# Spectral gated mix on one core: branch weights in 18 strided transfers each, and the l = 512 row placed by one transfer

## The chip, the cores and the metric

The kernel runs on one core of a Trainium2 chip. The metric is the device time of one execution in microseconds (us). Three runs of the kernel before gave 218.82, 219.64 and 219.72 us, median 219.64. The profile is of one execution of 218.76 us, whose instructions span 217.0 us.

## What is computed

Both branches take the same input x of 2048 rows and 1024 columns, in bf16. Each multiplies its 2-D real Fourier transform by its own complex weights (2048 x 513) and transforms back; a gate per row, from x and gate_w, mixes the two results.

```python
g = sigmoid((x * gate_w).sum(-1, keepdims=True))
X = rfft2(A_x)                                  # 2048 x 513 complex
a = irfft2(X * (A_w_r + 1j * A_w_i)).astype(bf16)
b = irfft2(X * (B_w_r + 1j * B_w_i)).astype(bf16)
return g * a + (1 - g) * b
```

## The kernel before, in words

The row index is n = 16 n1 + n2, and a frequency is k = k1 + 128 k2. Real input makes the frequencies k1 and 128 - k1 a pair, so 64 values of k1 are computed. A group `kg` (16 of them) takes four k1, their four mirrors and all 16 k2, which are 128 frequencies, one on each partition. Column frequencies l run from 0 to 512; 512 of them are handled as full rows of 512, and l = 512 on its own.

All instructions are recorded by the class `Sched` in program order, one list for each engine; an instruction waits on the semaphores of what it depends on, by keys of its reads and writes, and each engine works its list strictly in order. Evacuations of PSUM (`ev`, lines 290 to 298) go to ScalarE (ACT) or VectorE (DVE), whichever has the smaller sum of estimated costs so far.

1. Fold and first transform (lines 376 to 404). For each pair of n2, DVE folds the columns of x (`fold`, 8 instructions of 128x1024), TensorE (PE) transforms over n1 with the table F, ACT evacuates into R3 (`Z`). The gate's row sums are collected through R2 and end as the small tile ZG.
2. The first large loop (`for t in range(21)`, lines 524 to 543). At step t, PE runs `stage_d(t)` (columns, table DM), `stage_s2(t-1)` (over n2, result `X` in R4) and `stage_i1(0, t-5)` (inverse over k2 of branch 0). Every second step DVE makes one `prod` (line 443): the complex product of two groups with the branch's weights, two multiplies of 128x2048 and two of 128x1024. At t = 17 and 19 the row l = 512 is handled: `p512` (line 478) multiplies it with column 512 of the weights, which touches every group of the branch, `v512` (line 490) transforms it on PE. At t = 18 and 20 `prod` already works on branch 1. `v512_row(0)` (line 500) follows the loop.
3. The second large loop (lines 558 to 568): `stage_i1(1, t)` of branch 1, its products, `stage_dinv(0, t-3)` (inverse over columns of branch 0), the gate's weights (`gmix`), and at t = 15 `v512_row(1)`.
4. The last loop (lines 598 to 602): `stage_dinv(1, t)` and `s1inv(t-1)`: the last inverse with the mix of both branches, an evacuation, four DVE instructions of 128x512 and the store.

Weights. `wload(b, kgs)` (line 332) fills WR[b] group by group: real and imaginary part, 64 partitions with one row of 513 elements each, and again for the mirror; group 0 needs four transfers of 16 rows for its mirror half because of the row 64. That makes 70 transfers on SyncE's queue (SP) for each branch. In branch 1 every group also writes the keys `zrow` and `gwt`, because WR[1] is the same memory (R2) that the gate used; so each group waits for the group before it. Group kg holds the k1 from 4 kg to 4 kg + 3, at partition 64 pm + 4 k2 + ii (pm is the mirror half, ii the place in the group).

The row l = 512. `v512(b)` leaves its result in V5 as 16 partitions (kg) of 128 elements (16 q2 by 8). It has to stand in partition 0 of VR[b] in the order q2, kg, 8. `v512_row(b)` does that with 16 transfers, one for each kg, after all groups of the branch have been evacuated (`("V", b, k)`). `stage_dinv(b, 0)` waits for it (key `Vf`).

SP's list is, in order: x, the tables, the weights of branch 0, those of branch 1, the tables DI and RM, `v512_row(0)`, `v512_row(1)`, 16 stores.

```python
dma("sp", prs, [], [("W", b, kg)] + (["zrow", "gwt"] if b else []))   # line 352
r = ["X5"] + [("W", b, k) for k in range(16)]                         # line 483, p512
[("V5", b)] + [("V", b, k) for k in range(16)], [("Vf", b)])          # line 503, v512_row
```

Of the kernel before, what the change touches and what calls it, by code (L numbers as in the profile page):

```python
# [7 lines left out]
AP = bass.AP  # L8
BF = dt.bfloat16

NS = 514
# [9 lines left out]
def make_consts():  # L21


    C = {}
    pi2 = 2 * np.pi
    n1 = np.arange(128)[:, None, None]
    n2 = np.arange(16)[None, :, None]
    k1 = np.arange(64)[None, None, :]
    a = pi2 * ((16 * n1 * k1 + n2 * k1) % 2048) / 2048.0
    F = np.zeros((128, 16, 64, 2))  # L30
    F[..., 0] = np.cos(a)
# [34 lines left out]
    for z in range(2):  # L66
        for pm in range(2):
            for k2 in range(16):
                for ii in range(4):
                    i = ii if pm == 0 else 3 - ii  # L70
                    po = pm * 64 + k2 * 4 + ii
                    spec = (z == 1 and i == 0)
                    for q2 in range(16):
                        w = np.exp(-1j * pi2 * q2 * (k2 + (1 if (pm == 1 and not spec) else 0)) / 16)
                        if spec and pm == 1:
                            w = w * np.exp(-1j * pi2 * q2 * 64 / 2048)
                        r0, r1 = q2 * 8 + i * 2, q2 * 8 + i * 2 + 1
                        wr, wi = w.real, w.imag
                        if spec:
                            r = r0 if pm == 0 else r1  # L80
                            S2[z, 0, r, po] = wr
                            S2[z, 1, r, po] = wi
                        else:
                            sg = 1.0 if pm == 0 else -1.0
                            S2[z, 0, r0, po] = wr
                            S2[z, 0, r1, po] = -sg * wi
                            S2[z, 1, r0, po] = wi
                            S2[z, 1, r1, po] = sg * wr
                        cr, ci = wr, -wi
                        K = KI[z, :, po, :, q2, i, :]  # L90
                        if spec:
                            ri = pm
                            K[0, 0, ri], K[1, 0, ri] = cr, -ci
                            K[0, 1, ri], K[1, 1, ri] = ci, cr
                        else:
                            K[0, 0, 0], K[1, 0, 0] = cr, -ci
                            K[0, 0, 1], K[1, 0, 1] = -sg * ci, -sg * cr
                            K[0, 1, 0], K[1, 1, 0] = ci, cr
                            K[0, 1, 1], K[1, 1, 1] = sg * cr, -sg * ci
        S2[z, 2] = -S2[z, 1]  # L100
# [6 lines left out]
    one = np.zeros((128, 2))  # L107
    one[0] = 1.0
    C["ONE"] = one
    return C  # L110


# [118 lines left out]
def bass_gated_mix__spectral_gfnet__spectral_gfnet__prompt_kernel(  # L231
# [24 lines left out]
    RM = sb("RM", 2048)  # L256
    GS = sb("GS", 16)
    ONE = sb("ONE", 2)
    RING = sb("RING", 11264)
    GROW = sb("GROW", 512)  # L260
    X5 = sb("X5", 32)
# [54 lines left out]
        dma(eng, [(ap(t, 0, [[1, n]]).bitcast(dt.uint16), cst[key].ap())], [], [key])  # L316


    XCH = [(0, 2), (2, 4), (4, 8), (8, 12), (12, 16)]
    cload("act", FM, "F", 2048)  # L320
    for a, b in XCH[:2]:
        dma("sp", [(ap(R1, a * 1024, [[1024, b - a], [1, 1024]]), xv[:, a:b, :])], [], [("x", i) for i in range(a, b)])
    dma("act", [(ap(R2, 2048, [[1, 1024]], 0, 1), gate_w.rearrange("(o d) -> o d", o=1))], [], ["gw"])
    cload("act", ONE, "ONE", 2)
    for a, b in XCH[2:]:
        dma("sp", [(ap(R1, a * 1024, [[1024, b - a], [1, 1024]]), xv[:, a:b, :])], [], [("x", i) for i in range(a, b)])
    cload("sp", DM, "DM", 2048)
    cload("sp", S2, "S2", 768)
    cload("sp", KI, "KI", 1024)
    cload("sp", GS, "GS", 16)  # L330

    def wload(b, kgs):
        for kg in kgs:
            prs = []
            T = WR[b]
            for c in range(2):
                src = wsrc[b][c]
                off = kg * 2 * NS + c * NS
                n = src.shape[-1]

                def rows(r0, k2n, inn, p0):
                    return AP(src.tensor, src.offset + r0 * n, [[128 * n, k2n], [n, inn], [1, n]])
                prs.append((ap(T, off, [[1, n]], 0, 64), rows(4 * kg, 16, 4, 0)))
                if kg:
                    prs.append((ap(T, off, [[1, n]], 64, 64), rows(125 - 4 * kg, 16, 4, 64)))
                else:
                    for ii in range(4):
                        r0 = 125 + ii if ii < 3 else 64
                        P = pit[id(T)]
                        prs.append((AP(T, (64 + ii) * P + off, [[4 * P, 16], [1, n]]),  # L350
                                    AP(src.tensor, src.offset + r0 * n, [[128 * n, 16], [1, n]])))
            dma("sp", prs, [], [("W", b, kg)] + (["zrow", "gwt"] if b else []))
    wload(0, range(16))


    def fold(n, src, soff, tmp, st, dst, doff, p0, np_, ns, reads, skey, writes):
# [86 lines left out]
    def prod(b, m):  # L443

        T = WR[b]
        x = ap(R4, 2 * m * 1024, [[1024, 2], [512, 2], [1, 512]])
        w = ap(T, 2 * m * 2 * NS, [[2 * NS, 2], [NS, 2], [1, 512]])
        ws = ap(T, 2 * m * 2 * NS + NS, [[2 * NS, 2], [-NS, 2], [1, 512]])
        r = [("X", 2 * m), ("X", 2 * m + 1), ("W", b, 2 * m), ("W", b, 2 * m + 1)]
        p = PO + m % 2 * 2048  # L450
        dve(1230, tt(ap(RING, TO, [[1024, 2], [512, 2], [1, 512]]), x, w, ALU.mult), r, ["t0"])
        dve(1230, tt(ap(RING, TO + 2048, [[1024, 2], [512, 2], [1, 512]]), x, ws, ALU.mult), r, ["t1"])
        for c, op in enumerate((ALU.subtract, ALU.add)):
            t = TO + 2048 * c
            dve(680, tt(ap(RING, p + c * 512, [[1024, 2], [1, 512]]), ap(RING, t, [[1024, 2], [1, 512]]),
                        ap(RING, t + 512, [[1024, 2], [1, 512]]), op), [f"t{c}"], [("P", m % 2, c)])

    VR = {0: R1, 1: R5}

    def stage_i1(b, kg):  # L460
# [8 lines left out]
        S.op("pe", fns, [("P", kg // 2 % 2, 0), ("P", kg // 2 % 2, 1), "KI"], [("ps", s)])  # L469
        w = [("V", b, kg)]  # L470
        if kg == 0:
            w += allx if b == 0 else [("W", 0, k) for k in range(16)]
        ev(1024, ap(VR[b], kg * 8, [[128, 128], [1, 8]]), pslot(s, 0, [[8, 128], [1, 8]]), [("ps", s)], w)

    def x512():
# [2 lines left out]
    def p512(b):  # L478
# [1 line left out]
        x = ap(X5, 0, [[16, 2], [1, 16]])  # L480
        w = ap(T, 512, [[NS, 2], [2 * NS, 16]])
        ws = ap(T, NS + 512, [[-NS, 2], [2 * NS, 16]])
        r = ["X5"] + [("W", b, k) for k in range(16)]
        dve(100, tt(ap(P5, o, [[16, 2], [1, 16]]), x, w, ALU.mult), r, [("p5", b, 0)])
        dve(100, tt(ap(P5, o + 32, [[16, 2], [1, 16]]), x, ws, ALU.mult), r, [("p5", b, 1)])
        for c, op in enumerate((ALU.subtract, ALU.add)):
# [3 lines left out]
    def v512(b):  # L490
# [6 lines left out]
        S.op("pe", fns, [("P5", b, 0), ("P5", b, 1), "KI"], ["m7"])  # L497
        ev(128, ap(V5, b * 128, [[1, 128]], 0, 16), misc(7, 0, [[1, 128]], 16), ["m7"], [("V5", b)])

    def v512_row(b):  # L500
        dma("sp", [(ap(VR[b], 2048 + 8 * k, [[128, 16], [1, 8]], 0, 1), ap(V5, b * 128, [[8, 16], [1, 8]], k, 1))
                   for k in range(16)],
            [("V5", b)] + [("V", b, k) for k in range(16)], [("Vf", b)])

    def stage_dinv(b, n2):
        s = slot()
# [17 lines left out]
    for t in range(16 + 5):  # L524
# [5 lines left out]
            stage_i1(0, t - 5)  # L530
        if t >= 2 and t % 2 == 0:
            prod(t // 18, t // 2 - 1 - t // 18 * 8)
        if t == 3:
            wload(1, range(16))
            cload("sp", DI, "DI", 2048)
            cload("sp", RM, "RM", 2048)
        if t == 17:
# [95 lines left out]
```

## Time and profile before

| what | value |
|---|---|
| median of three runs | 219.64 us (218.82 to 219.72) |
| profiled execution | 218.76 us, of which 217.0 us span |
| PE, DVE, ACT busy | 60%, 55%, 56% of the span |
| PE weight loads busy | 42% |
| granted TensorE clock, mean | 0.842 of full speed |
| DMA, mean over the span | 90 GB/s |
| chain that ended last | SP issue 19%, DMA of in_B_w_i 17% |

How to read it: the page of the profile cuts the span into 40 slices of 5.4 us. There, PE, DVE and ACT are at eight to ten tenths between slices 8 and 14, stand at 0 from slice 16 to slice 22 (about 81 to 122 us), and are busy again to the end but for a gap at slices 31 and 32. The views by waits, by engine and by time say what each gap waits for. SPq is SP's queue of transfers: a row of it is the time that issuing took, not the time of the data.

### The profile page before, as it was taken

The numbers are of one execution on the slowest core, as the hardware profiler recorded it, in microseconds if no ns is written. First come the engines' busy times: TensorE is split into PE (matmuls) and PEld (weight loads), VectorE is DVE, ScalarE is ACT, GpSimd is POOL, SyncE is SP. The second block draws the span as 40 slices with busy tenths as digits, with TensorE's granted clock in tenths as the row PEclk, the third lists the DMA queues.
The fourth block names the chain that finished last, engine by engine and source line by source line (L and its number), as shares of the span: only waits on it lengthen the run. The fifth ranks groups of instructions, "written<-read, shape, count | busy, mean of one in ns | idle before, by whom it ended". The sixth has DMA issues, their size and how long they took to land.

```text
span 217.0 us, 2645 instructions
## 1 busy us (share of the span) xinstructions
PE 129.6 (60%) x999; PEld 91.4 (42%) x1008; DVE 120.3 (55%) x193; ACT 120.6 (56%) x130; POOL 0.2 (0%) x4
## 2 busy tenths in 40 slices
PE   0368777999999960000000284499799029998970
PEld 0255435666777640000000153388687016665530
DVE  0999900489988870000000399753971203989995
ACT  2258966998998961000000035189999104898870
POOL 0000000000000000000000000000000000000000
PEclk9999999999999985555555558799999856999996
DMA  6999344343112221222222510000000000233243
GB/s 224 354 416 268 97 100 109 85 107 91 36 52 63 61 72 49 66 76 52 62 74 58 194 48 1 3 0 0 0 3 0 1 0 3 97 145 146 100 179 112
DMA packets 15647, 19.55 MB, mean 90 GB/s; under 512 B 3985, under 2 KB 12305, under 8 KB 15250
## 3 DMA queue, kind: packets, MB, share of 16 engines
q1 hardware_dynamic: 15344, 18.85, 28.2%
q10 hardware_dynamic: 290, 0.53, 0.7%
q8 instruction: 8, 0.13, 0.2%
q14 instruction: 5, 0.04, 0.1%
HBM read 15.16 MB, written 4.19 MB: 89 GB/s over the span
## 4 chain that ended last, share of the span: by engine, by line
ACT 24%; DMA 20%; SPq 19%; DVE 17%; PE 12%; issue 7%; DVEq 0%
SPq L313 19%; DMA R<-in_B_w_i_dram 17%; ACT R L296 13%; PE PS L307 12%; DVE RING L310 9%; ACT RING L296 9%; DVE R L310 5%; DMA R<-in_A_x_dram 2%; DVE RING L298 2%; ACT GROW L551 1%; DMA R<-V 1%; ACT L551 1%; DVE P L310 0%; DVEq L209 0%
## 5 line engine op out<-in xcount | busy, mean ns | idle before, releaser
L296 ACT ACTIVATE R<-PS 128x1024 bf16<-128x1024 f32 (+1 forms) x80 | 76.1, 1035 | 27.2 <-PE PS L307 27.2
L310 DVE TENSOR_TENSOR RING<-R 128x2048 bf16<-128x2048 bf16 (+1 forms) x48 | 48.0, 1040 | 14.2 <-ACT R L296 8.4
L296 ACT ACTIVATE RING<-PS 128x1024 bf16<-128x1024 f32 x40 | 43.0, 1133 | 19.6 <-PE PS L307 19.6
L310 DVE TENSOR_TENSOR RING<-RING 128x512 bf16<-128x512 bf16 (+1 forms) x96 | 44.5, 508 | 7.4 <-PE PS L307 4.1
L307 PE MATMUL PS<-DI,R 128*128 128x256 bf16 x256 | 35.3, 286 | 16.6 <-DMA R<-V 9.3
L307 PE MATMUL PS<-KI,RING 128*128 128x256 bf16 x256 | 36.6, 294 | 5.2 <-DVE RING L310 3.2
L307 PEld LDWEIGHTS PS<-DI,R 128*128 128x128 bf16 x256 | 25.4, 102 | 25.4 <-issue 15.8
L307 PEld LDWEIGHTS PS<-KI,RING 128*128 128x128 bf16 x256 | 25.2, 105 | 13.2 <-DVE RING L310 4.0
L307 PE MATMUL PS<-KI,P 128*16 128x128 bf16 (+1 forms) x8 | 1.2, 303 | 42.2 <-DVE P L310 42.2
L310 DVE TENSOR_TENSOR P<-X,R 128x32 bf16<-128x32 bf16 x4 | 0.7, 212 | 43.0 <-DMA R<-in_B_w_i_dram 43.0
L296 ACT ACTIVATE V<-PS 16x128 bf16<-16x128 f32 x2 | 0.5, 258 | 42.1 <-PE PS L307 42.1
L307 PE MATMUL PS<-FM,R 128*128 128x128 bf16 x128 | 11.6, 263 | 13.3 <-DVE R L310 13.3
L307 PEld LDWEIGHTS PS<-KI,P 128*16 128x16 bf16 (+1 forms) x8 | 0.6, 109 | 42.8 <-issue 42.8
L307 PE MATMUL PS<-DM,R 128*128 128x256 bf16 x128 | 16.5, 273 | 0.3 <-ACT RING L296 0.2
L307 PE MATMUL PS<-RING,S 128*128 128x1 bf16 (+2 forms) x91 | 15.8, 304 | 1.3 <-ACT RING L296 1.1
L298 DVE CAST RING<-PS 128x1024 bf16<-128x1024 f32 x8 | 10.0, 1248 | 11.6 <-PE PS L307 11.6
L307 PEld LDWEIGHTS PS<-FM,R 128*128 128x128 bf16 x128 | 9.9, 120 | 15.1 <-DVE R L310 14.7
L307 PEld LDWEIGHTS PS<-DM,R 128*128 128x128 bf16 x128 | 11.8, 98 | 3.0 <-ACT RING L296 1.1
L307 PEld LDWEIGHTS PS<-RING,S 128*128 128x128 bf16 x96 | 7.8, 97 | 7.5 <-ACT RING L296 1.4
L310 DVE TENSOR_TENSOR R<-RING 128x1024 bf16<-128x1024 bf16 x16 | 10.3, 688 | 0.3
L307 PE MATMUL PS<-R,FM 128*128 128x512 bf16 x30 | 9.4, 388 | 0.7 <-ACT RING L296 0.4
L307 PE MATMUL PS<-RING,DM 128*128 128x512 bf16 x30 | 9.4, 391 | 0.1
(23 smaller groups left out, 37.3 us busy)
## 6 DMA issues: line engine op xcount, KB each, us to landing
out_dram<-RING SPq DMA_DIRECT2D x16, 256.0 KB, 2.0
R<-in_A_x_dram SPq DMA_DIRECT2D x3, 1024.0 KB, 10.9
R<-in_A_w_r_dram SPq DMA_DIRECT2D x31, 64.1 KB, 2.3
R<-in_A_w_i_dram SPq DMA_DIRECT2D x31, 64.1 KB, 2.3
R<-in_B_w_r_dram SPq DMA_DIRECT2D x31, 64.1 KB, 2.2
R<-in_B_w_i_dram SPq DMA_DIRECT2D x31, 64.1 KB, 2.2
R<-in_A_x_dram SPq DMA_DIRECT2D x2, 512.0 KB, 5.5
FM<-c_F ACTq DMA_DIRECT2D x1, 512.0 KB, 4.8
```

The lines of the kernel that those rows point to most:

```text
L296: S.op("act", lambda e: e.activation(outap, inap, ACT.Copy), reads, writes)
L298: S.op("dve", lambda e: e.tensor_copy(outap, inap), reads, writes)
L307: return lambda e: e.matmul(o, l, r, start=start, stop=stop, skip_group_check=True)
L310: return lambda e: e.tensor_tensor(out=o, in0=a, in1=b, op=op)
L313: S.op(eng, [lambda e, d=d, s=s: e.dma_start(d, s) for d, s in pairs], reads, writes, dma=kind)
L551: S.op("act", lambda e: e.activation(ap(GROW, 0, [[1, 512]]), misc(7, 0, [[1, 512]]), ACT.Sigmoid), ["m7"], ["GROW"])
```

## The change

- Weights: one recorded transfer group for each branch, made of 18 transfers. For each partition place in a block of eight (pm, ii) and each of real and imaginary part, one transfer fills 16 partitions (one for each k2, eight apart) with all 16 groups: 16 x 16 rows of 513 elements. The place pm = 1, ii = 3 is split in two, because of the row 64. The key is now `("W", b)` for a whole branch: a product of two groups waits for all of it. The keys `zrow` and `gwt` are written once.
- To make that a regular stride, group kg now holds the k1 kg, kg + 16, kg + 32 and kg + 48, and the partition is 8 k2 + 4 pm + ii. The tables F, RM, S2 and KI are permuted accordingly; sizes and counts of matmuls stay.
- The row l = 512: after V5, eight small matmuls with an identity (ID) and one more evacuation bring it to V6, as 16 partitions (q2) of 128 elements, for each branch; then one transfer places it.
- F moves from ACT's queue to SP's, behind the first transfer of x. `wload(1)` is recorded at t = 0 and not at t = 3.

```diff
-    k1 = np.arange(64)[None, None, :]
+    kord = (np.arange(16)[:, None] + 16 * np.arange(4)[None, :]).reshape(-1)
+    k1 = kord[None, None, :]
...
-                    po = pm * 64 + k2 * 4 + ii
+                    po = k2 * 8 + pm * 4 + ii
...
+    xload(0, 2)
+    cload("sp", FM, "F", 2048)
...
-    wload(0, range(16))
+    cload("sp", ID, "ID", 16)
+
+    def wload(b):
+
+        prs = []
+        T = WR[b]
+        P = pit[id(T)]
+        for pm in range(2):
+            for ii in range(4):
+                for c in range(2):
+                    src = wsrc[b][c]
+                    n = src.shape[-1]
+
+                    def part(r0, step, k0, k1):
+                        prs.append((AP(T, (4 * pm + ii) * P + (2 * k0 + c) * NS, [[8 * P, 16], [2 * NS, k1 - k0], [1, n]]),
+                                    AP(src.tensor, src.offset + r0 * n, [[128 * n, 16], [step * n, k1 - k0], [1, n]])))
+                    if pm == 0:
+                        part(16 * ii, 1, 0, 16)
+                    elif ii < 3:
+                        part(80 + 16 * ii, -1, 0, 16)
+                    else:
+                        part(127, -1, 1, 16)
+                        part(64, 1, 0, 1)
+        dma("sp", prs, [], [("W", b)] + (["zrow", "gwt"] if b else []))
+    wload(0)
...
-        r = [("X", 2 * m), ("X", 2 * m + 1), ("W", b, 2 * m), ("W", b, 2 * m + 1)]
+        r = [("X", 2 * m), ("X", 2 * m + 1), ("W", b)]
...
+        fns = [mm(misc(7, j * 16, [[1, 16]], 16), ap(V5, b * 128 + j, [[8, 16]], 0, 16), ap(ID, 0, [[1, 16]], 0, 16), True, True)
+               for j in range(8)]
+        S.op("pe", fns, [("V5", b), "ID"], ["m7"])
+        ev(128, ap(V6, b * 128, [[1, 8], [8, 16]], 0, 16), misc(7, 0, [[16, 8], [1, 16]], 16), ["m7"], [("V6", b)])
+
     def v512_row(b):
-        dma("sp", [(ap(VR[b], 2048 + 8 * k, [[128, 16], [1, 8]], 0, 1), ap(V5, b * 128, [[8, 16], [1, 8]], k, 1))
-                   for k in range(16)],
-            [("V5", b)] + [("V", b, k) for k in range(16)], [("Vf", b)])
+        dma("sp", [(ap(VR[b], 2048, [[128, 16], [1, 128]], 0, 1), ap(V6, b * 128, [[1, 128]], 0, 16))],
+            [("V6", b)] + [("V", b, k) for k in range(16)], [("Vf", b)])
...
-        if t == 3:
-            wload(1, range(16))
+        if t == 0:
+            wload(1)
```

How the order of instructions moves, at three places. First SP, where the weights of branch 1 begin; s_pe is PE's semaphore, s_d28 and s_d29 are those of the first two groups of branch 1. Before:

```order
L313 DMA R<-in_A_w_i_dram 64x1x513 x2
L313 DMA R<-in_B_w_r_dram 64x1x513 [waits s_pe]
L313 DMA R<-in_B_w_r_dram 16x513 x4
L313 DMA R<-in_B_w_i_dram 64x1x513
L313 DMA R<-in_B_w_i_dram 16x513 x4
L313 DMA R<-in_B_w_r_dram 64x1x513 [waits s_d28]
L313 DMA R<-in_B_w_r_dram 64x1x513
L313 DMA R<-in_B_w_r_dram 64x1x513 [waits s_d29]
```

And now, from the end of branch 0 to the start of branch 1:

```order
L319 DMA R<-in_A_w_r_dram 16x15x513
L319 DMA R<-in_A_w_r_dram 16x513
L319 DMA R<-in_A_w_i_dram 16x15x513
L319 DMA R<-in_A_w_i_dram 16x513
L319 DMA R<-in_B_w_r_dram 16x16x513 [waits s_pe]
L319 DMA R<-in_B_w_i_dram 16x16x513
L319 DMA R<-in_B_w_r_dram 16x16x513
```

The wait for PE stays; the 15 waits of a group for the one before it are gone.

Second PE, at the row l = 512 (P holds its products, V its transform), between `stage_i1(0, 14)` and `stage_i1(0, 15)`. Before:

```order
L307 MATMUL PS<-KI,P 16x128 [waits s_dve]
L307 MATMUL PS<-KI,P 16x128
L307 MATMUL PS<-KI,P 1x128 x2
L307 MATMUL PS<-KI,P 16x128 [waits s_dve,s_act]
L307 MATMUL PS<-KI,RING 128x256 x8
```

And now:

```order
L313 MATMUL PS<-KI,P 16x128 [waits s_dve]
L313 MATMUL PS<-KI,P 16x128
L313 MATMUL PS<-KI,P 1x128 x2
L313 MATMUL PS<-ID,V 16x16 [waits s_d12,s_act]
L313 MATMUL PS<-ID,V 16x16 x7
L313 MATMUL PS<-KI,P 16x128 [waits s_dve,s_act]
L313 MATMUL PS<-ID,V 16x16 [waits s_act]
L313 MATMUL PS<-KI,RING 128x256 x8
```

PE, which works in order, waits for two more evacuations by ACT in each branch before it comes to `stage_i1(0, 15)`.

Third DVE, at the start of the last loop; a CAST is an evacuation that fell to DVE. Before:

```order
L310 TENSOR_TENSOR DM<-RM,FM 128x512
L298 CAST R<-PS 128x1024
L298 CAST RING<-PS 128x1024
L310 TENSOR_TENSOR RING<-RING 128x512
L310 TENSOR_TENSOR RING<-RING 128x2x256 x3
L298 CAST RING<-PS 128x1024
```

And now:

```order
L316 TENSOR_TENSOR DM<-RM,FM 128x512
L304 CAST R<-PS 128x1024
L304 CAST RING<-PS 128x1024 x2
L316 TENSOR_TENSOR RING<-RING 128x512
L316 TENSOR_TENSOR RING<-RING 128x2x256 x3
```

The two added evacuations shift the balance of `ev`: two evacuations of the last loop stand ahead of DVE's first block of four, and three instead of four stand behind it.

## Rows read from the trace of the kernel before

**Rows 1.** Waits of the run: engine, line, waited for, us in total, times, longest
```profile
DVE P L310 <- DMA R<-in_B_w_i_dram: 43.0, 1, 43.0
...
PE PS L307 <- DMA R<-V: 9.3, 1, 9.3
```

**Rows 2.** DVE in time, around the products of l = 512: start, us, instruction
```profile
122.87 0.34 DVE L310 TENSOR_TENSOR P<-X,R 128x32 bf16<-128x32 bf16 x2 [42.95 <-DMA R<-in_B_w_i_dram]
...
123.34 2.35 DVE L310 TENSOR_TENSOR RING<-R 128x2048 bf16<-128x2048 bf16 x2
```

**Rows 3.** SP's queue in time: first weights of branch 1, and the table behind them
```profile
51.93 3.14 SPq L313 DMA_DIRECT2D R<-in_B_w_r_dram  x5
...
121.24 0.58 SPq L313 DMA_DIRECT2D DI<-c_DI  x1
```

**Rows 4.** SP's issues of line 313: count, ns least/median/most, first and last start
```profile
L313 SPq DMA_DIRECT2D R<-in_A_w_r_dram x35: 582/594/1384, 5.4 to 49.6; - x35
...
L313 SPq DMA_DIRECT2D R<-V x32: 497/589/592, 127.1 to 175.8; - x32
```

**Rows 5.** DMA issues: count, KB each, median us from issue to landing
```profile
R<-in_B_w_r_dram SPq DMA_DIRECT2D x31, 64.1 KB, 2.2
...
KI<-c_KI SPq DMA_DIRECT2D x1, 256.0 KB, 13.9
...
R<-in_B_w_r_dram SPq DMA_DIRECT2D x4, 16.0 KB, 2.3
```

**Rows 6.** Stretches of time: busy by engine, then PEclk, DMA share, GB/s
```profile
4.00:5.00 1.00, 0.00 (x0) 0.00 (x0) 0.00 (x0) 0.00 (x0) 0.00 (x0) 1.00 1.04 422
...
19.00:20.00 1.00, 1.00 (x7) 0.42 (x6) 1.00 (x3) 1.00 (x2) 0.00 (x0) 1.00 1.27 201
...
26.00:30.00 4.00, 2.82 (x31) 1.74 (x29) 1.52 (x3) 3.69 (x5) 0.00 (x0) 1.00 0.43 103
```

**Rows 7.** DVE in time: the first fold, and the first product of branch 0
```profile
5.78 1.29 DVE L310 TENSOR_TENSOR RING<-R 128x1024 bf16<-128x1024 bf16 x2 [5.78 <-DMA R<-in_A_x_dram]
...
40.90 2.36 DVE L310 TENSOR_TENSOR RING<-R 128x2048 bf16<-128x2048 bf16 x2 [6.41 <-ACT R L296]
```

**Rows 8.** PE and ACT in time, where the first large loop meets the second
```profile
80.80 0.60 PE L307 MATMUL PS<-KI,P 128*16 128x128 bf16 x4
...
124.08 1.89 PE L307 MATMUL PS<-KI,RING 128*128 128x256 bf16 x8
...
138.34 1.86 PE L307 MATMUL PS<-DI,R 128*128 128x256 bf16 x8 [5.57 <-issue]
...
140.24 1.02 ACT L296 ACTIVATE R<-PS 128x1024 bf16<-128x1024 f32 x1 [6.37 <-PE PS L307]
```

**Rows 9.** Groups by line, kept apart by form: count, busy us, mean ns
```profile
L307 PE MATMUL PS<-ONE,R 1*128 1x1 bf16 x24 | 0.9, 160 | 0.7 <-ACT R L296 0.7
...
L296 ACT ACTIVATE V<-PS 16x128 bf16<-16x128 f32 x2 | 0.5, 258 | 42.1 <-PE PS L307 42.1
...
L298 DVE CAST RING<-PS 128x1024 bf16<-128x1024 f32 x8 | 10.0, 1248 | 11.6 <-PE PS L307 11.6
```

**Rows 10.** SP and PE in time, where the second large loop meets the last
```profile
127.06 10.05 SPq L313 DMA_DIRECT2D R<-V  x16
...
165.55 2.88 PE L307 MATMUL PS<-DI,R 128*128 128x256 bf16 x24 [0.27 <-ACT R L296]
...
166.44 9.98 SPq L313 DMA_DIRECT2D R<-V  x16
...
177.69 3.57 PE L307 MATMUL PS<-DI,R 128*128 128x256 bf16 x16 [9.26 <-DMA R<-V]
```

**Rows 11.** The chain that ended last, its piece between SP's last issue and PE
```profile
175.82 1.73 DMA R<-V
```

**Rows 12.** DVE's first block of the last loop, and the stretch from there
```profile
183.91 1.55 DVE L310 TENSOR_TENSOR RING<-RING 128x512 bf16<-128x512 bf16 x4 [1.38 <-ACT RING L296]
...
183.91:214.04 30.13, 24.62 (x160) 15.43 (x161) 28.16 (x68) 23.62 (x25) 0.00 (x0) 0.99 0.34 126
```

More of the change, by code (lines that the diff above doesn't have):

```diff
@@ L109, in make_consts @@
     C["ONE"] = one
+    idt = np.zeros((128, 16))
+    idt[:16] = np.eye(16)
+    C["ID"] = idt
     return C
@@ L258, in bass_gated_mix__spectral_gfnet__spectral_gfnet__prompt_kernel @@
     ONE = sb("ONE", 2)
+    ID = sb("ID", 16)
+    V6 = sb("V6", 256)
     RING = sb("RING", 11264)
@@ L316, in cload, with xload @@
         dma(eng, [(ap(t, 0, [[1, n]]).bitcast(dt.uint16), cst[key].ap())], [], [key])
-    XCH = [(0, 2), (2, 4), (4, 8), (8, 12), (12, 16)]
-    cload("act", FM, "F", 2048)
-    for a, b in XCH[:2]:
+    def xload(a, b):
         dma("sp", [(ap(R1, a * 1024, [[1024, b - a], [1, 1024]]), xv[:, a:b, :])], [], [("x", i) for i in range(a, b)])
+    xload(0, 2)
+    cload("sp", FM, "F", 2048)
     dma("act", [(ap(R2, 2048, [[1, 1024]], 0, 1), gate_w.rearrange("(o d) -> o d", o=1))], [], ["gw"])
     cload("act", ONE, "ONE", 2)
-    for a, b in XCH[2:]:
-        dma("sp", [(ap(R1, a * 1024, [[1024, b - a], [1, 1024]]), xv[:, a:b, :])], [], [("x", i) for i in range(a, b)])
+    for a, b in ((2, 4), (4, 8), (8, 12), (12, 16)):
+        xload(a, b)
     cload("sp", DM, "DM", 2048)
@@ L330, in bass_gated_mix__spectral_gfnet__spectral_gfnet__prompt_kernel @@
     cload("sp", GS, "GS", 16)
[L332 to L352, printed above, removed]
-    wload(0, range(16))
+    cload("sp", ID, "ID", 16)
[20 more added lines that the diff above has]
+    wload(0)
     def fold(n, src, soff, tmp, st, dst, doff, p0, np_, ns, reads, skey, writes):
@@ L471, in stage_i1 @@
         if kg == 0:
-            w += allx if b == 0 else [("W", 0, k) for k in range(16)]
+            w += allx if b == 0 else [("W", 0)]
         ev(1024, ap(VR[b], kg * 8, [[128, 128], [1, 8]]), pslot(s, 0, [[8, 128], [1, 8]]), [("ps", s)], w)
@@ L482, in p512 @@
         ws = ap(T, NS + 512, [[-NS, 2], [2 * NS, 16]])
-        r = ["X5"] + [("W", b, k) for k in range(16)]
+        r = ["X5", ("W", b)]
         dve(100, tt(ap(P5, o, [[16, 2], [1, 16]]), x, w, ALU.mult), r, [("p5", b, 0)])
```

## The prediction

> **What bounds the kernel now.** I read the list of waits first [rows 1]. One wait stands out: DVE sits idle for 43.0 us, once, for a transfer of B's imaginary weights. DVE in time shows the place [rows 2]: the products of the row l = 512 for branch 1 start at 122.87, after 42.95 us of idle time, so DVE had been free since 79.92. These small products need column 512 of all sixteen groups of B's weights, and the large products of branch 1 stand behind them on DVE. SP's queue says why the weights are late [rows 3]: B's 70 transfers are issued from 51.93 to 121.24, 69.3 us. One issue takes a median of 0.594 us [rows 4], 0.63 with the gap to the next; 70 of them are 44 us, and the other 25 us are the 15 waits of a group for the landing of the one before. They begin at 51.93 because A's 70 issues stand ahead.
>
> Then I looked where PE idles afterwards. The first place is 5.57 us ahead of the first inverse over columns of branch 0, at 138.34 [rows 8]; SP issues the 16 small transfers of the l = 512 row just then, from 127.06 to 137.11 [rows 10]. The second is 9.26 us at 177.69, where the trace names that transfer itself [rows 1, 10]. From 183.91 DVE is busy 28.16 of 30.13 us [rows 12]: it bounds the last loop. So three stretches wait for issues on SP, and the rest is compute.
>
> **The change part by part.** All times are on the clock of before, against the profiled execution: 218.76 us, of which 217.0 are span.
>
> *Start.* The first fold waits until 5.78 for x [rows 7], while 0.52 MB of x and 0.52 MB of F travel together from two queues. With F behind that part of x, x lands earlier by at most F's 0.52 MB at 422 GB/s [rows 6], 1.25 us. Folds bound this phase, so all of it moves: -1.2; bounds 0 and -1.25.
>
> *A's weights.* 18 issues replace 70, but the first product now needs the whole branch, 2 x 2048 x 513 x 2 B = 4.20 MB. It starts at 40.90 now, 39.7 after the gain above [rows 7]. What stands ahead in the queue lands at 18.3 (KI, issued at 4.41, takes 13.9 [rows 5]). For the rate there are two rows [rows 6]: a trickle of 103 GB/s keeps the DMA engines busy 0.43 of the time, which scales to 240 GB/s; the short backlog at 19 to 20 us moves 201 GB/s at a share over 1. That gives 17.5 to 20.9 us and A's weights at 35.8 to 39.2. I take 0; the cover is 0.5 to 3.9 us, and if it is gone the delay goes through, since the inverse of branch 0 follows the first product on PE at once. Bounds 0 and +7 (150 GB/s; see the rivals). SP's issues hide behind the data unless one takes over (35.8 - 6.2) / 18 = 1.6 us; no row has 256 rows in one transfer, those there take 0.59 [rows 4]. ID's and F's issues on SP, under 0.6 us each, are hidden with them.
>
> [...]
>
> *B's weights.* They wait for the same PE instruction, now reached as soon as A's issues end (about 18 us) and that instruction is done, before 34. Their data follow A's, 17.5 to 20.9 us more: 53 to 60. DVE comes for them at 78.7. The whole 42.95 us go: **-42.95**. Bounds: 18 us of margin, so nothing less unless the rate is below about half of what I take. DI and RM follow at 65 and are needed after 90.
>
> *The added transposes.* For each branch eight tiny matmuls (0.16 us each at most [rows 9], overlapped: 0.4 us for eight) and an evacuation of 0.26 us [rows 9], with two hand-overs between PE and ACT. PE passes them in order, ahead of the last inverse group of branch 0. From the start of the first l = 512 transform at 80.80 [rows 8] I count: transform to 81.4, V at 82.1 (ACT is busy until then), transposes and V6 to 82.85, second transform and V to 83.8, second transposes to 84.3. That group begins at 84.4, where the old one, shifted by 42.95, would begin at 124.08 - 42.95 = 81.13 [rows 8]: 3.3 us later. DVE's second product of branch 1 reaches the buffer which that group frees at 86.2, so DVE loses nothing.
>
> *Row l = 512 of branch 0.* The last group is evacuated by 87.3; one issue and landing take 1.73 from the start of the issue [rows 11], so the row stands at 89.1, before PE asks at about 92. The 5.57 us of idle time go, the 3.3 us of delay come in: 2.3 us. [...] The evacuation at 140.24, 97.29 when shifted, comes at 92 to 93: **-4.8**; bounds -2.3 and -6.4 (the whole of ACT's 6.37 [rows 8]). From there on ACT bounds the loop, as before.
>
> *Row l = 512 of branch 1.* SP starts at 166.44 [rows 10]; the last of its 16 issues starts at 175.82 [rows 11]. One transfer lands at 168.2, when PE ends the batch begun at 165.55 (168.43 [rows 10]). The 9.26 us go. [...] One evacuation of 1.25 us [rows 9] moves from behind DVE's first block to ahead of it, where it partly replaces ACT's; DVE bounds what is behind [rows 12]. I take 0.5 of it: **-11.5**; bounds -9.3 and -12.3.
>
> *Sum.* -1.2 - 42.95 - 4.8 - 11.5 = -60.45: 218.76 becomes 158.3. The median of the runs is 0.9 above the profiled execution, so I say **159.0**.
>
> **The rivals.**
>
> 1. *A's weights are late.* The wait for a whole branch takes the place of sixteen early ones. It decides below 4.20 MB / (39.7 - 18.3) = 196 GB/s. At 150 GB/s A lands at 46.3 and the time is 165.6; at 175, 161.6. For it: the 201 GB/s of the backlog [rows 6]. Against it: that second mixes large and small rows. Chance 0.20, at 161 to 167.
>
> 2. *The second half gives less.* Between the loops ACT and DVE may hold what PE gains, and the added hand-overs may cost more. With the lower bounds of both terms, -2.3 and -9.3, and nothing at the start, the time is 218.76 - 54.55 = 164.2. Chance 0.12.
>
> 3. *Slower: a transfer of 16 partitions is dealt to few DMA engines.* 240 GB/s over 16 engines is 15 GB/s for one. Two branches of 4.20 MB on k engines take 560/k us after 18.3, and from B's landing the rest is 217 - 122.87 less the 16.3 of the last two terms, 78 us, with 1.8 outside the span. It is slower than before when 560/k exceeds 121, so for four engines or fewer: 238 us at k = 4, some 660 at one. For it: nothing in these rows excludes it for 16 rows, since 16 KB land in 2.3 us [rows 5] and one engine would need only 1.1. Against it: 64 KB land in 2.2 [rows 5] where one engine would need 4.3, so such transfers are spread, and the 16-row ones differ only in the count. Chance 0.04. [...]
>
> 4. *The wait for B's weights stays in other words*, because something orders the transfers still. The new order on SP has one wait ahead of B's 18, for PE, and none between them. Chance 0.01, at about 202.5, the two row terms alone (218.76 - 16.3).
>
> **How the numbers follow.** My case has 0.63, at 155.5 to 161. The range 155.5 to 166.0 takes it with rival 2 and most of rival 1; left out are what is quicker than the bounds, very late weights, and rivals 3 and 4, under 0.2 together. A measurement of this kernel can tell about 0.5% from no change. Faster by more than that: 0.95; within it 0.01; slower 0.04 (rival 3).
>
> **What would show it.** In the list of waits DVE's 43.0 us for in_B_w_i is gone, and so are PE's 9.3 us for V. SP issues 36 weight transfers of about 0.6 us, B's from about 33 us. The first 128x2048 product stands at 39.7 and is released by ACT; if it is released by a transfer of in_A_w, rival 1 holds, and its idle time is the price. The first column inverse of branch 0 follows its predecessor without a gap, as does that of branch 1. The mean clock rises over 0.842. A wait of DVE for B's weights, however short, makes the part on B wrong; transfers that land one engine at a time make all of it wrong.

## The result, and the profile after

The changed kernel ran in 161.62 us (median of four runs, 160.53 to 165.54) beside 219.58 us for the kernel before. The ratio is 0.735, with a 95% interval from 0.728 to 0.741; the ratios here leave out executions that were slower at a lower granted clock, such as that of 165.54 us. The forecast was 159.0, with a range from 155.5 to 166.0. The profiled execution took 160.53 us, of which 159.0 are span; the mean granted clock rose from 0.842 to 0.968.

The list of waits of the changed kernel (engine, line, waited for: us in total, times, longest) no longer has either row of [rows 1]. A new one stands near its head:

```profile
DVE RING L316 <- DMA R<-in_A_w_i_dram: 10.2, 1, 10.2
```

DVE in time (start, us, instruction, and in brackets the idle time before it with what ended it) shows where that wait is, what became of the one for B, and the start:

```profile
4.32 1.29 DVE L316 TENSOR_TENSOR RING<-R 128x1024 bf16<-128x1024 bf16 x2 [4.32 <-DMA R<-in_A_x_dram]
...
8.17 1.29 DVE L316 TENSOR_TENSOR RING<-R 128x1024 bf16<-128x1024 bf16 x2 [1.23 <-DMA R<-in_A_x_dram]
...
44.59 2.36 DVE L316 TENSOR_TENSOR RING<-R 128x2048 bf16<-128x2048 bf16 x2 [10.21 <-DMA R<-in_A_w_i_dram]
...
82.37 0.34 DVE L316 TENSOR_TENSOR P<-X,R 128x32 bf16<-128x32 bf16 x2
...
82.83 0.34 DVE L316 TENSOR_TENSOR P<-X,R 128x32 bf16<-128x32 bf16 x2
```

Branch 1's products of l = 512 stand at 82.83 instead of 122.87 [rows 2], right behind those of branch 0 and without a wait. But the first large product, at 40.90 and released by ACT before [rows 7], is now at 44.59 and released by A's weights. The first fold is 1.46 us earlier than in [rows 7], and the second pair of folds, behind it, now waits for x. Before, it did not:

```profile
8.31 1.28 DVE L310 TENSOR_TENSOR RING<-R 128x1024 bf16<-128x1024 bf16 x2
```

So only 0.14 us is left of that gain.

SP's queue in time shows the issues that [rows 3] and [rows 10] showed before:

```profile
6.34 0.68 SPq L319 DMA_DIRECT2D R<-in_A_w_r_dram  x1
7.06 3.66 SPq L319 DMA_DIRECT2D R<-in_A_w_i_dram  x1
...
34.19 0.57 SPq L319 DMA_DIRECT2D R<-in_B_w_r_dram  x1
...
56.74 0.58 SPq L319 DMA_DIRECT2D DI<-c_DI  x1
...
90.34 30.31 SPq L319 DMA_DIRECT2D R<-V  x2
```

B's issues run from 34.19 to 56.7, where they ran from 51.93 to 121.24. The two transfers of the l = 512 row replace 32 (the last line spans both, at 90.34 and about 120.1). The first A transfer issues in 0.68 us and the second in 3.66, though both have 256 rows. A's 18 issues run from 6.34 to 32.45, 26.1 us; their 4.20 MB take 24.9 at the rate below, so on the whole the issues go at about the pace of the data.

The stretch in which the weights travel says how fast that is (columns as in [rows 6]: busy by engine, PEclk, DMA share, GB/s):

```profile
20.00:40.00 20.00, 16.31 (x151) 9.88 (x151) 7.50 (x13) 15.07 (x18) 0.00 (x0) 1.00 1.14 169
```

That is 169 GB/s with the DMA engines busy throughout (a share of 1.14). Last, PE in time at the l = 512 row, and the clock in the same stretch:

```profile
82.51 1.05 PE L313 MATMUL PS<-KI,RING 128*128 128x256 bf16 x8 [1.96 <-DVE RING L316]
...
84.82 0.43 PE L313 MATMUL PS<-ID,V 16*16 16x16 bf16 x8 [0.94 <-ACT V L302]
86.06 0.59 PE L313 MATMUL PS<-KI,P 128*16 128x128 bf16 x4 [0.82 <-ACT V L302]
87.01 0.43 PE L313 MATMUL PS<-ID,V 16*16 16x16 bf16 x8 [0.36 <-ACT V L302]
87.37 6.15 PE L313 MATMUL PS<-KI,RING 128*128 128x256 bf16 x40
93.36 1.04 PE L313 MATMUL PS<-DI,R 128*128 128x256 bf16 x8
...
119.23 4.67 PE L313 MATMUL PS<-DI,R 128*128 128x256 bf16 x40 [0.26 <-ACT R L302]
```

```profile
82.00:84.00 2.00, 1.37 (x12) 0.90 (x12) 2.00 (x10) 0.40 (x1) 0.00 (x0) 0.97 0.00 0
84.00:86.00 2.00, 0.43 (x8) 0.34 (x8) 2.00 (x3) 1.48 (x3) 0.00 (x0) 0.50 0.00 0
...
88.00:90.00 2.00, 2.00 (x11) 1.40 (x10) 1.75 (x3) 0.91 (x2) 0.00 (x0) 0.50 0.00 0
90.00:92.00 2.00, 2.00 (x17) 1.63 (x16) 2.00 (x4) 1.38 (x3) 0.00 (x0) 0.82 0.02 2
```

Neither the first inverse over columns (93.36, 5.57 us of idle time in [rows 8]) nor the batch of 40 that contains the start of branch 1's (119.23, 9.26 us in [rows 10]) waits for the row. But three hand-overs between PE and ACT, 0.94, 0.82 and 0.36 us, stand between the tiny matmuls, and the granted clock falls there to 0.50 from about 84 to 90. The kernel before has no transposes, and its clock falls at this place too, right behind the same pause of PE for DVE:

```profile
79.52 1.35 PE L307 MATMUL PS<-KI,RING 128*128 128x256 bf16 x8 [1.96 <-DVE RING L310]
```

```profile
80.00:85.00 5.00, 1.39 (x10) 0.63 (x7) 0.00 (x0) 1.17 (x2) 0.00 (x0) 0.51 0.26 67
```

### The profile page after: what moved, and what is told of

The parts are those of the page before. It is cut to its first block, busy times and chain, and to the rows that moved or that the text cites. A ratio compares the mean times of both kernels' runs of the same rounds, so it can differ in the third digit from the quotient of the medians.

```text
span 159.0 us, 2541 instructions
## 1 busy us (share of the span) xinstructions
PE 124.6 (78%) x1015; PEld 90.0 (57%) x1024; DVE 120.4 (76%) x193; ACT 121.7 (77%) x132; POOL 0.2 (0%) x4
## 4 chain that ended last, share of the span: by engine, by line
ACT 37%; PE 27%; DVE 22%; issue 7%; DMA 4%; SPq 1%; DVEq 0%
PE PS L313 27%; ACT R L302 21%; ACT RING L302 13%; DVE RING L316 12%; DVE R L316 6%; DMA R<-in_A_x_dram 4%; DVE RING L304 4%; ACT GROW L564 1%; ACT L564 1%; ACT V L302 1%; SPq L319 1%; DVEq L213 0%
## 5 line engine op out<-in xcount | busy, mean ns | idle before, releaser
L313 PE MATMUL PS<-KI,RING 128*128 128x256 bf16 x256 | 34.0, 281 | 7.5 <-issue 3.1
L313 PE MATMUL PS<-DI,R 128*128 128x256 bf16 x256 | 32.7, 273 | 1.5 <-DVE RING L304 1.2
L313 PEld LDWEIGHTS PS<-KI,RING 128*128 128x128 bf16 x256 | 24.3, 101 | 14.0 <-issue 3.9
L313 PEld LDWEIGHTS PS<-DI,R 128*128 128x128 bf16 x256 | 24.4, 98 | 8.4 <-DVE RING L304 2.2
L313 PE MATMUL PS<-R,G 128*1 128x512 bf16 x32 | 7.5, 378 | 0.7 <-ACT R L302 0.7
L304 DVE CAST R<-PS 128x1024 bf16<-128x1024 f32 x4 | 4.9, 1223 | 3.1 <-PE PS L313 3.1
L313 PEld LDWEIGHTS PS<-RING,DM 128*128 128x128 bf16 x32 | 3.1, 98 | 3.8
```

Source lines behind the costliest of these rows:

```text
L304: S.op("dve", lambda e: e.tensor_copy(outap, inap), reads, writes)
L313: return lambda e: e.matmul(o, l, r, start=start, stop=stop, skip_group_check=True)
```

## The experiments

Three things needed a test: why A's weights come at 169 GB/s, what each part of the change is worth, and what the hand-overs on PE cost. "First product" is the first 128x2048 instruction on DVE that reads A's weights; each span is set against the profiled one of 159.0 unless another is named. The experiments ran on three chips, and where no range of times is given it is one execution. Beside them the kernel before took 219.29 to 222.16 us, so a difference of one or two us between spans of different chips shows little by itself.

**Loading A in two halves.** Branch A is loaded as groups 0 to 7, then 8 to 15, each with its own key, so that the first product waits for half.

```diff
-        dma("sp", prs, [], [("W", b)] + (["zrow", "gwt"] if b else []))
+        for h in (range(2) if b == 0 else (None,)):
...
+            keys = [("W", b, 0), ("W", b, 1)] if h is None else [("W", b, h)]
+            dma("sp", prs, [], keys + (["zrow", "gwt"] if b else []))
```

> Branch 0's weights in two recorded loads (groups 0 to 7, then 8 to 15; 34 transfers of 16 partitions by 8 groups), so that a product waits for half a branch only. Theory (the whole-branch wait for A's weights costs what the first product of branch 0 lost, 44.59 against some 40.8): the first half lands at about 18.3 + 2.1 MB / 168 GB/s = 31, the first product starts at 40.5 to 41 and is released by ACT, and the profiled span falls by 3.5 to 4 us from 159.0, to 155 to 155.5. Rival (the lateness is made up later, because DVE has slack in that loop): the first product moves, the span stays within 1 us of 159. Second rival (36 issues by 16 more cost as much again): the first half lands after 40.5.

Measured: 158.62 us (158.20 to 159.10), ratio 0.719 [0.717, 0.721], span 157.3. The first product is released by ACT again, so the wait for the whole branch did cause the delay:

```profile
41.10 2.36 DVE L316 TENSOR_TENSOR RING<-R 128x2048 bf16<-128x2048 bf16 x2 [6.42 <-ACT R L302]
```

Yet the end comes only 1.7 us earlier, not the 3.5 of the product (the spans of the four executions are 156.4 to 157.3). The clock and PE in time of this kernel show why, next to the rows above:

```profile
80.00:82.00 2.00, 1.73 (x12) 0.88 (x9) 2.00 (x8) 0.76 (x1) 0.00 (x0) 0.55 0.00 0
...
88.00:90.00 2.00, 2.00 (x11) 1.44 (x10) 2.00 (x3) 1.02 (x1) 0.00 (x0) 0.50 0.02 2
```

```profile
79.73 1.47 PE L313 MATMUL PS<-KI,RING 128*128 128x256 bf16 x8 [1.95 <-DVE RING L316]
81.13 0.59 PE L313 MATMUL PS<-KI,P 128*16 128x128 bf16 x4
82.46 0.43 PE L313 MATMUL PS<-ID,V 16*16 16x16 bf16 x8 [0.74 <-ACT V L302]
...
85.02 7.17 PE L313 MATMUL PS<-KI,RING 128*128 128x256 bf16 x40
92.02 1.04 PE L313 MATMUL PS<-DI,R 128*128 128x256 bf16 x8
```

The clock falls earlier, at 80 instead of 84, and is still at 0.50 until 90. It falls behind the pause of 1.95 us, within the batch of 79.73 and ahead of the first hand-over. That batch is 2.78 us earlier than in the changed kernel, the first inverse over columns only 1.34: the same 40 matmuls take 7.17 us instead of 6.15, and about half of the gain is returned in this stretch.

**What sets the rate: order, partitions, alignment.** Four kernels change only how the weights are addressed; the second and the fourth leave them at other frequencies than they belong to, so they serve for the times alone. The first alternates the two mirror halves, so that a transfer to partitions 8 k2 + ii is followed by one to 8 k2 + 4 + ii:

```diff
-        for pm in range(2):
-            for ii in range(4):
-                for c in range(2):
+        for ii in range(4):
+            for c in range(2):
+                for pm in range(2):
```

> The same 18 transfers in another order: the two mirror halves (pm) alternate, so that neighbouring transfers lie on partitions that differ in bit 2. [...] Theory pieces (168 GB/s is what pieces of 1026 bytes give at full load): 167 GB/s and 44.6 stay in any case.

The second loads the same bytes by transfers of 128 partitions with two rows each:

```diff
+        for c in range(2):
...
+                prs.append((AP(T, (4 * h + c) * NS, [[P, 128], [2 * NS, 2], [1, n]]),
+                            AP(src.tensor, src.offset + 2 * h * n, [[16 * n, 128], [n, 2], [1, n]])))
```

> [...] Changed in the computation: the weights stand at other frequencies than they belong to. [...] Theory pieces: 167 GB/s as before, first product at 44 to 45.

The third leaves the transfers and makes the pitch of a row in the tile 528 elements, a multiple of 32 bytes:

```diff
-NS = 514
+NS = 528
```

> The rows of the weights stand 528 elements apart in SBUF and not 514, so that each piece starts at a multiple of 32 bytes there; sources, transfers and counts as in the changed kernel. [...]

The fourth puts each transfer's 16 partitions next to each other:

```diff
-                        prs.append((AP(T, (4 * pm + ii) * P + (2 * k0 + c) * NS, [[8 * P, 16], [2 * NS, k1 - k0], [1, n]]),
+                        prs.append((AP(T, (4 * pm + ii) * 16 * P + (2 * k0 + c) * NS, [[P, 16], [2 * NS, k1 - k0], [1, n]]),
```

> As the changed kernel, sources, counts and pieces the same, but each transfer fills 16 adjacent partitions and not 16 that are eight apart. Changed in the computation: the weights stand at other frequencies than they belong to. [...] Theory source (168 GB/s is due to the sources, 16 places 131 KB apart in memory): 168 GB/s stays, span 159 to 160.

The stretch from 20 to 40 us for alternating halves:

```profile
20.00:40.00 20.00, 17.38 (x146) 9.61 (x146) 7.57 (x13) 13.99 (x17) 0.00 (x0) 1.00 1.13 208
```

For 128 partitions, two shorter stretches, one with A's weights on the way and one with B's (from 20 to 40 there is a pause between them):

```profile
20.00:25.00 5.00, 4.78 (x43) 2.61 (x42) 4.93 (x9) 3.46 (x5) 0.00 (x0) 1.00 1.10 349
...
42.00:48.00 6.00, 5.51 (x43) 3.34 (x43) 5.39 (x7) 6.00 (x8) 0.00 (x0) 1.00 1.10 353
```

For 16 adjacent partitions, the same stretch, and DVE at the first product:

```profile
20.00:40.00 20.00, 17.61 (x145) 9.58 (x144) 7.97 (x14) 13.99 (x17) 0.00 (x0) 1.00 1.14 100
```

```profile
62.77 2.36 DVE L316 TENSOR_TENSOR RING<-R 128x2048 bf16<-128x2048 bf16 x2 [27.26 <-DMA R<-in_A_w_i_dram]
```

The share is 1.10 to 1.14 in all of them, so the DMA engines are equally occupied and the bytes are not. With the pitch of 528 it is 167 GB/s (a share of 1.13), the first product at 44.90 and the time 160.83: this alignment has no part in it. The source rows of the adjacent kernel are those of the changed one, so 100 against 169 comes from the destination's partitions alone. For the 349 to 353 of 128 partitions that is not separated, because its source rows lie differently too. (The adjacent kernel took 181.38 us.) Alternating halves gave 159.51 us with the first product at 41.53, released by ACT; 128 partitions gave 158.51 with it at 40.99. Those two and the halves end within 1.5 us of each other in span (158.0, 156.5, 157.3), and behind the first product they differ in little: it stands at 40.99 to 41.53 in all three.

So at about the same share the rate was 100, 169 or 349 to 353 GB/s; what in the hardware makes the difference is not shown. The two sets of alternating halves lie four partitions apart, and alternating them gained 23% (208 against 169). Why it is 208 and not 350 stays open.

**The l = 512 row.** First the changed kernel with the old 16 transfers for each branch, without V6 and its transposes:

```diff
-        dma("sp", [(ap(VR[b], 2048, [[128, 16], [1, 128]], 0, 1), ap(V6, b * 128, [[1, 128]], 0, 16))],
-            [("V6", b)] + [("V", b, k) for k in range(16)], [("Vf", b)])
+        dma("sp", [(ap(VR[b], 2048 + 8 * k, [[128, 16], [1, 8]], 0, 1), ap(V5, b * 128, [[8, 16], [1, 8]], k, 1))
+                   for k in range(16)],
+            [("V5", b)] + [("V", b, k) for k in range(16)], [("Vf", b)])
```

> The row l = 512 again by 16 transfers for each branch, without the transposes and V6; the weights as in the changed kernel. Theory (the two row terms are worth what the profile of the change shows, 94.1 us from the branch-1 products of l = 512 to the end before, 76.2 now, 17.9 less): PE waits 4 to 6 us ahead of the first column inverse of branch 0 and about 9 us ahead of that of branch 1, and the profiled span is 174 to 177. Rival (most of what came behind the weights is PE's clock, which no longer falls to its lower level for 40 us): the span is 165 to 170.

Measured: 182.63 us, span 180.9, so undoing the row costs 21.9 us, more than either theory said. PE in time of this kernel:

```profile
100.96 1.87 PE L313 MATMUL PS<-DI,R 128*128 128x256 bf16 x8 [7.30 <-issue]
102.61 1.91 PE L313 MATMUL PS<-KI,RING 128*128 128x256 bf16 x8
...
141.49 3.57 PE L313 MATMUL PS<-DI,R 128*128 128x256 bf16 x16 [9.55 <-DMA R<-V]
```

Both waits of [rows 8, 10] are back, the first longer than before (7.30 against 5.57), and with them the batches of 8 at a granted clock of 0.50 (100 to 105), in 1.87 and 1.91 us instead of 1.04. Its l = 512 products of branch 1 stand at 84.19, 1.4 us later than in the changed kernel, which is part of the 21.9. From there to the end it takes 180.9 - 84.2 = 96.7 us.

The clock falls in this kernel too, which has no transposes and one hand-over here, but for about 3 us and not 7:

```profile
86.18 0.59 PE L313 MATMUL PS<-KI,P 128*16 128x128 bf16 x4 [0.94 <-ACT V L302]
```

```profile
86.00:88.00 2.00, 1.82 (x11) 1.23 (x12) 2.00 (x3) 0.39 (x2) 0.00 (x0) 0.50 0.00 0
```

Then the other way round: the kernel before with this part alone.

> The kernel before with its 70 weight transfers for each branch, and only the l = 512 row changed: transposes, V6 and one transfer. Theory (the row terms hold by themselves): span 217.0 - 16 to 18 = 199 to 201, DVE still waits about 43 us for B's weights. Rival (as undoing the row showed, it is worth 21.9): span 195.

Measured: 201.56 us, span 199.8, or 17.2 less than before. DVE still waits for B, somewhat longer than in [rows 2]:

```profile
124.32 0.34 DVE L315 TENSOR_TENSOR P<-X,R 128x32 bf16<-128x32 bf16 x2 [44.66 <-DMA R<-in_B_w_i_dram]
```

From there to the end it takes 199.8 - 124.3 = 75.5 us, where the kernel before takes 217.0 - 122.9 = 94.1 and the changed one 159.0 - 82.8 = 76.2. So from these products on the part is worth 18.6 us in the kernel before, and 96.7 - 76.2 = 20.5 in the changed one. The products stand 1.4 us later in this kernel and in the one with the old row, which makes 17.2 of the first and 21.9 of the second.

**The 15 waits of B's groups.** The kernel before, with only group 0 writing the shared keys:

```diff
-            dma("sp", prs, [], [("W", b, kg)] + (["zrow", "gwt"] if b else []))
+            dma("sp", prs, [], [("W", b, kg)] + (["zrow", "gwt"] if b and kg == 0 else []))
```

> The kernel before, 70 transfers for each branch, but only the first group of branch 1 writes the keys zrow and gwt, so the 15 waits of a group for the one before it are gone and the issues remain. Theory (44 us of issue and 25 us of waits add up): B's issues end at 52 + 70 x 0.634 = 96.4, the products of l = 512 for branch 1 start at 98 to 99 and not at 122.9, the span is 192 to 194. [...]

Measured: 196.20 us, span 194.4. DVE in time:

```profile
100.05 0.34 DVE L310 TENSOR_TENSOR P<-X,R 128x32 bf16<-128x32 bf16 x2 [20.27 <-DMA R<-in_B_w_i_dram]
```

The wait shrinks from 42.95 to 20.27 us, and the span by 22.6, to a little above the 192 to 194 of the theory. The data do not bound it now: B's issues run from 52.1 to 98.2 at about 0.6 us each, and the DMA engines are busy less than half of the time (a share of 0.42 from 70 to 80 and 0.47 from 80 to 90). (Beside this run the kernel before took 222.16 us, 26.0 more than this one; the wait in the trace, 22.7 shorter, speaks for the smaller figure.) So of the change's 58.0 us of span, 22.6 need only this one condition. The step from there to 18 transfers gives 13.5 (194.4 to 180.9, the experiment with the old row): 20.27 of the wait are gone, but the products stand only 15.9 us earlier (100.05 against 84.19), since A's weights are late, and what follows takes 2.4 us longer.

**F's place.** The halves, with F on ACT's queue again, as before the change:

```diff
-    cload("sp", FM, "F", 2048)
+    cload("act", FM, "F", 2048)
```

> The kernel with A's weights in two halves (first experiment), and F back on ACT's queue beside the first transfer of x. Theory (the move of F gains nothing, since the second pair of folds then waits for x behind F): the first fold starts at 5.5 to 6 and not at 4.3, the second pair at 8.2 to 8.5 without a wait, the first product at 41 +- 0.5, span 157.3 +- 0.7. Rival (the move is worth its 1.2 us): the first product at 42.3, span 158.5.

Measured: 157.79 us, span 156.0. The first fold starts at 5.60, the second pair at 8.14 without a wait, and the first product at 40.75. With F behind x these were 4.22, 8.50 and 41.10 in the kernel of halves. Moving F gained nothing.

**The same kernels on another chip, and the transposes moved.** The changed kernel again, the halves with F on ACT again, and that kernel with the transposes of both branches taken out of `v512` and put behind the first large loop; they use another PSUM area, so PE goes on with `stage_i1(0, 15)` while ACT evacuates V5.

```diff
+    def v512t(b):
...
-        S.op("pe", fns, [("V5", b), "ID"], ["m7"])
-        ev(128, ap(V6, b * 128, [[1, 8], [8, 16]], 0, 16), misc(7, 0, [[16, 8], [1, 16]], 16), ["m7"], [("V6", b)])
+        S.op("pe", fns, [("V5", b), "ID"], [("mt", b)])
+        ev(128, ap(V6, b * 128, [[1, 8], [8, 16]], 0, 16), misc(7 - b, M7B, [[16, 8], [1, 16]], 16), [("mt", b)], [("V6", b)])
...
+    v512t(0)
+    v512t(1)
     v512_row(0)
```

> The changed kernel again, for its scatter beside the next two on the same chip. Theory (its first product waits for A's weights, so their rate is in its time): 160.5 to 165.5 us again, a spread of over 1%. Rival (that spread was one of the chip it ran on): all within 0.5%.

> A's weights in two halves and F on ACT's queue, as in the seventh experiment, timed. Theory (no wait for A's weights is left and F's move bought nothing): 157 to 158.5 us, spread below 0.5%, 2 to 4 us below the changed kernel. Rival (the 156.0 us span of one look was luck with PE's clock): 158.5 to 159.5, as the halves alone.

> As the one before, but both l = 512 transforms go to different PSUM banks and the transposes come after the last inverse group of branch 0, so that PE passes that group without four hand-overs to ACT. [...] Rival (DVE's second product of branch 1, which ends at 87.3, and a sparse PE hold it): the first column inverse at 90 to 90.7 and less than 0.7 us gained.

| kernel | median us (lowest to highest) | ratio to before [95%] |
|---|---|---|
| changed kernel | 163.03 (160.98 to 165.02) | 0.739 [0.733, 0.745] |
| halves, F on ACT | 159.25 (158.08 to 159.36) | 0.725 [0.722, 0.728] |
| and transposes later | 157.36 (156.89 to 158.10) | 0.718 [0.715, 0.721] |

PE in time of the last one, and the clock in the stretches where it was 0.50 above:

```profile
79.33 1.05 PE L313 MATMUL PS<-KI,RING 128*128 128x256 bf16 x8 [1.95 <-DVE RING L316]
80.31 0.61 PE L313 MATMUL PS<-KI,P 128*16 128x128 bf16 x8
80.86 1.05 PE L313 MATMUL PS<-KI,RING 128*128 128x256 bf16 x8
81.83 0.69 PE L313 MATMUL PS<-ID,V 16*16 16x16 bf16 x16
83.73 1.92 PE L313 MATMUL PS<-KI,RING 128*128 128x256 bf16 x16 [1.20 <-DVE RING L316]
87.20 1.92 PE L313 MATMUL PS<-KI,RING 128*128 128x256 bf16 x16 [1.55 <-DVE RING L316]
88.96 1.04 PE L313 MATMUL PS<-DI,R 128*128 128x256 bf16 x8
```

```profile
84.00:86.00 2.00, 1.65 (x16) 1.23 (x13) 2.00 (x3) 1.34 (x3) 0.00 (x0) 1.00 0.02 2
...
88.00:90.00 2.00, 2.00 (x19) 1.54 (x16) 2.00 (x4) 1.71 (x2) 0.00 (x0) 1.00 0.00 0
```

The tiny matmuls stand in two runs without a hand-over, the clock stays at 1.00 in this profile, though the pause of 1.95 us is there too, and the first inverse over columns starts at 88.96 (92.24 in the kernel without this step). That is 1.9 us in the medians, and this version beats both the kernel before and the changed one.

Not all of it is the step's. The halves with F on ACT took 159.25 us, in the range of the rival and above the 157.79 of their first execution; in three of these four executions the mean clock was 0.94, and in the profiled one it was low from 15 to 25 us, long before the row (see the end). From branch 1's l = 512 products to the end the last version takes 75.5 us, the one without the step 77.2 in this profile and 76.3 in the earlier one, so the step is worth about 1 to 2 us.

What brings the clock down is not shown. In ten of the other 13 profiles it falls from 1.00 to 0.50 between 0.5 and 2.9 us after PE's pause of 1.94 to 1.96 us for DVE (by the means of the stretches), also in the three without transposes at that place (the kernel before, the old row, the one without the 15 waits). In the other three (alternating halves, pitch of 528, 16 adjacent partitions) the times point the same way: behind the same pause of 1.95 us, 40 matmuls take 7.41, 6.16 and 6.79 us, where 40 take 4.67 at a clock of 1.00 (119.23 in the changed kernel). In four (the kernel before, the halves, alternating halves, the halves with F on ACT) PE slows down ahead of any transposes: the batch of 8 behind the pause takes 1.24 to 1.47 us instead of 1.05. In the last version PE works without a stop for 3.2 us behind it. But its mean clock is 0.994, 0.979, 0.996 and 0.969 in the four executions, the two lower ones 0.9 and 1.2 us longer in span, so in two of them it fell somewhere, and only the first was profiled.

The changed kernel scatters over 4 to 5 us in both sets of executions, and the versions in which nothing waits for A's weights over 0.9 to 1.3. In the second profile of it the first product is 0.9 us later and the l = 512 products 2.1 us later than in the first, which is most of the 2.5 us between the two spans. What varies there was not settled.

## Why the prediction held, and which of its terms did not

The sum forecast a span of 217.0 - 60.45 = 156.55; it was 159.0. Two stretches separate the terms. Up to branch 1's l = 512 products the change was to save 1.2 + 42.95 = 44.15 us and saved 122.87 - 82.83 = 40.04. From there to the end it was to save 16.3 and saved 94.13 - 76.17 = 17.96. So 4.1 us were lost and 1.7 won against the sum. Beyond the idle time, the -4.8 and the -11.5 also count a faster PE, 1.7 us of it in the second; no run shows the clock rates assumed for that. The runs show the granted share and the times: behind the two gaps 8 matmuls took 1.86 us at a share of 0.53 (138 to 141) and 16 took 3.57 at 0.50 (from 177.69) before, and now 8 take 1.04 and 40 take 4.67, which is 1.87 for 16, at 1.00. (Two sums of the prediction are off by a little: 158.3 and 0.9 make 159.2, where it says 159.0, and the outer bound of the last term is 9.26 + 1.7 + 1.25 = 12.2, where it says 12.3.)

**B's weights: right.** The whole wait is gone. The cover is large: DI's issue, which stands behind all of B's in the queue, is at 56.74, and DVE comes at 82.83. The adjacent kernel shows the cover's end: at 100 GB/s branch 1's products wait 1.30 us, though A's late weights bring DVE there only at about 103. I had put the limit at about half of the rate I took (201 to 240); 169 was still above it.

**Start: wrong, 1.2 us lost.** "Folds bound this phase, so all of it moves" failed. F was put between the first and the second part of x, so what the first fold gained (1.46 us, more than the 1.25 that I called the most) the second pair lost, 1.23 us of it as idle time at 8.17. ZG is at 34.20 instead of 34.3, and the run with F back on ACT confirms it.

**A's weights: wrong, some 2.9 us lost.** I took 0, from rates of 201 to 240 GB/s. The rate was 169, below the 196 that the text names as the point where rival 1 decides. Its arithmetic holds: 4.20 MB at 169 take 24.9 us, so A's weights are in at about 43.2 by its working, and the product stood at 44.59. The price shrinks on the way: the first product is 3.7 us later than before, the l = 512 products of branch 0 only 3.0 (82.37 against 79.38). What failed is the choice of rows. The 103 GB/s trickle at a share of 0.43 was scaled up as though the share measured a capacity that any transfer can use, but at a full share the rate here went from 100 to 353, by how the weights are addressed. The transfers behind both rows had mostly 64 partitions and went by turns to the partitions from 0 and those from 64 on; these have 16 and stay on one mirror half for eight or more in a row. No run separates the two differences, but alternating the halves alone gave 208, close to the 201 of the backlog.

**The added transposes: right in size, not all of it theirs.** PE comes to `stage_i1(0, 15)` at 87.37, 4.54 us after branch 1's products; before it was 1.21. The difference is 3.3 us, as predicted. In the changed kernel with the old row, which has no transposes, that group begins at 86.70, 2.51 us after the products, so about 2.0 of the 3.3 are the transposes'; the other 1.3 come because both branches' transforms now follow each other on PE. DVE lost 0.25 us by it (at 89.37), where I had expected no loss. The granted clock was 0.50 through the hand-overs (84 to 90); that the transposes bring it down is not shown, since it fell without them too.

**Row of branch 0: right in sign, too small.** Measured from branch 1's products to the batch that starts at 165.55 before and 119.23 now, this stretch is 42.68 - 36.40 = 6.3 us shorter; I said 4.8, bound 6.4. The first inverse over columns alone is 15.47 - 10.53 = 4.9 us earlier, where I had only 5.57 - 3.3 = 2.3: the 40 matmuls ahead of it take 5.99 us in one piece, where before they took 8.69 from 124.08 to 132.77, with a pause for DVE and at a clock of 0.50 until 131. PE, kept back by the hand-overs, found all its products ready, and the clock was back at 1.00 by 92. The other 1.3 are the two batches of 8 after the gap, 1.86 and 1.81 before and 1.04 now.

**Row of branch 1: right.** From that batch to the end it is 51.45 - 39.77 = 11.7 us, against 11.5. DVE bounds the last loop as before, busy 27.38 of the 29.57 us from 126.68.

**The rivals.** Rival 1 is what happened: by its working a rate of 169 gives 159.0 + 43.2 - 39.7 = 162.5 us, and 161.62 was measured. The median lies above my own case (155.5 to 161) and in rival 1's band, which I gave 0.20. That it is still within 3 us of the point forecast is luck in part: the rows' gain of 1.7 us has nothing to do with A's weights and the start, which lost 4.1. Rival 2 falls with the 17.96. Rival 3 falls with a share of 1.14 of all 16 engines; rival 4 with the missing wait.

## What to carry to other kernels

Before a strided load replaces a plain one, look for a row with the same destination partitions, and not only the same bytes: the rate of transfers to 16 partitions went from 100 to 169 GB/s with their spacing, and to 350 with 128 partitions (and other source rows), at the same DMA share. When one key replaces many, the first reader waits for the last byte (10.21 us here); two keys put that reader back in its place (41.10 instead of 44.59). A few tiny matmuls with a hand-over each stopped PE several times (0.94, 0.82 and 0.36 us): put them where PE has other work between them. That was worth 1 to 2 us here; how much of it is the clock stays open.

## What was not expected of the hardware

- In the changed kernel the issue of a transfer of 256 rows took 0.68 us for the first of A and 0.57 to 0.65 for the first four of B, behind a pause of SP's queue from 32.45 to 34.19; many behind these took 1.2 to 1.5, and the longest 3.66. What sets this is not shown, but an issue time read off such a queue is not the cost of an issue alone.
- Pauses of PE of 0.94, 0.82 and 0.36 us among tiny matmuls, behind one of 1.96, went with some 6 us at a granted clock of 0.50. With pauses of 1.95, 1.20 and 1.55 us between larger batches it stayed at 1.00 in the one profile of that version. But behind the first of these pauses it fell to 0.50 in ten other profiles, with transposes or without, so which pause does it is not shown.
- In the second profile of the halves with F on ACT the clock was also 0.66 from 15 to 25 us, where it was 1.00 in their first profile and in the changed kernel; PE was busy 1.92 of the 4 us from 12 to 16, against 2.21 in the changed kernel. The first product then stood at 41.31 instead of 40.75.
